# Two parities of a gated mix of attention and FFN: both projected first, or each followed by its own FFN, with weight parts kept in HBM

## The chip, the cores and the metric

The kernel runs on one core of one Trainium2 chip. That core has a matrix engine (PE, with its weight loads PEld), VectorE (DVE), ScalarE (ACT), GpSimd (POOL) and SyncE (SP), which only issues transfers here. Each engine takes its instructions in order and they meet through semaphores. Transfers run on 16 DMA engines; they are issued by SP, by POOL and, in the changed kernel, by ACT. The metric is the device time of one execution in microseconds (us), and the comparison is by the median of several runs.

## The reference

Input x has 2048 tokens of 512 channels, all float32. The output is `g * a + (1 - g) * b`, with attention a and FFN b both computed from x:

```python
x = A_x
g = _sigmoid((x * gate_w).sum(-1, keepdims=True))
# a: 32 heads of 16 channels; token s looks at s, s-2, s-4 ... s-14 (8 places, masked below 0)
logits = jnp.einsum("bhsd,bhswd->bhsw", q, kg) * scale
a = jnp.einsum("bhsw,bhswd->bhsd", softmax(masked logits), vg)  # back to (S, D), then @ wo
b = (_gelu(x @ w_gate) * (x @ w_up)) @ w_down     # F = 1792
out = g * a + (1 - g) * b
```

Since the places looked at are two apart, even and odd tokens never meet in attention. The kernel calls them parity 0 and 1, with 1024 tokens each.

## The kernel before

*Number form.* A float32 product is made of three matmuls of a reduced format: every operand is held as a high part and a low part (what the high part leaves), and high x high, low x high and high x low are added in PSUM. `split` makes the two parts: an ACT copy for the high one, a subtraction on DVE or POOL for the low one (L77). So each product of tiles is three matmuls, 512 columns wide unless said otherwise.

*Projections.* `project(par, cb)` makes, for the 8 token tiles of a parity, one of three column blocks of wqkv: block 0 and 2 are keys and queries of half the heads, block 1 the values of all heads and the gate's sum. `take` (L229) copies a bank of PSUM to SBUF (tags s and r, 3 and 2 buffers) and issues its stores to HBM on SP. The order is written out by hand at the file's end: (0,0), (1,0), (0,1), (1,1), (0,2), (1,2), then `ffn(0)` and `ffn(1)`. x of parity 1 is split and its sums are made early (`load_x1`); the results are put into HBM by POOL (`keep`, 28 stores) and read back by POOL in the first FFN's last step (`operands_1`, 14 reads of 512 KB).

*Attention* runs on DVE: per parity four units of 8 heads. A unit loads keys and queries, makes scores (L289, L291), masks them (a select on POOL, L294), takes the softmax (L302 to L312), multiplies by the values (L325 to L333), transposes, and stores its result to HBM (L340, tensor os, on SP). A generator `fill` holds all units, parity 0 first. `pull(n)` takes about n us of it in between the other work, at a lower priority (`BEHIND`), so that it fills DVE while PE works. The tile framework's scheduler then fixes the order on every engine.

*FFN.* `ffn(par)` goes over 14 blocks f of 128 hidden channels. A product of x with gate and up weights is arranged so that seven products of half size take the place of eight (`gate_up`): it needs sums of weight quarters and sums of x parts (s1 to s4). For each f:
- `fetch` reads gate and up weights (512 KB, tag raw, two buffers) and `fetch_d` the down weights (256 KB, tag r), both on POOL;
- `combine` (L404) forms the differences of quarters, three DVE instructions;
- `operands` makes the high and low parts of the seven weight operands (tags g0, g1, two buffers each): an ACT copy with sign minus into the low part (L420), an accumulating DMA from POOL that adds the raw weight (L421), and an ACT copy into the high part (L423);
- `down_w` splits the down weights, the subtraction on POOL (tag d);
- `gate_up` does the products (L435), copies and additions (L439, L444, L510), the gelu on ACT (L526, L544), the product of gate and up (L448) and its split (L450, L451; the subtraction on DVE for parity 0 and on POOL for parity 1);
- `down` multiplies by the down weights two f at a time (L474). Four token tiles stay in PSUM (`acc`), four go to SBUF and back (L468, L483).

The weights are read, combined and split for parity 0 and once more for parity 1 (`ahead`, `again` prepare f = 0 and 1 of the second FFN during the finish of the first).

*Finish.* The last `down` steps scale by 1 - g (L478), and `finish` adds attention's output times wo (L651) in the same PSUM banks, then copies to SBUF (L660, L662; tags s and rt) and stores the rows (L663, on POOL for parity 0 and SP for parity 1).

*What sets the order around the change:* one queue per engine, the hand-written calls at the end of the file, the scheduler's order within them, and the number of buffers of each tag (`BUFS`).

Of the kernel before, what the change touches and what calls it, by code (L numbers as in the profile page):

```python
# [15 lines left out]
P = 128  # L16
# [14 lines left out]
BT = 4  # L31
# [9 lines left out]
def tile_gated_mix(ctx: ExitStack, tc: tile.TileContext, xt, wqkv, wff, wo, out):  # L41
# [29 lines left out]

    def split(eng, hi, lo, raw, copy=None):
        if copy:
            copy(hi, raw)
        else:
            nc.scalar.activation(hi, raw, AF.Copy)  # L76
        eng.tensor_tensor(lo, raw, hi.bitcast(F32), op=OP.subtract)  # L77


    KS, VS, QS, OS = {}, {}, {}, {}  # L80
# [12 lines left out]
    X, WC = {}, {}  # L93

    def raws():
        for i in range(3):
            if i == 1:
                yield from (tl("c")[:, :512] for _ in range(4))
            else:
                t = tl("raw")  # L100
                yield from (t[:, n * 512:(n + 1) * 512] for n in range(4))

    early = raws()
    for blk in range(2):
        for kc in range(KC):
            X[0, blk, kc] = (tl("rt", F32R), tl("rt", F32R)) if blk and kc < 2 else pair("A")

    def load_xk(kc, blk, first=False):
        hi, lo = X[0, blk, kc]
        for a, n in ((0, P), (P, 512 - P)) if first else ((0, 512),):  # L110
            raw = next(early) if not a else raw
            c = slice(a, a + n)
            nc.sync.dma_start(raw[:, c], xt[blk, :, kc, c])
            split(nc.vector, hi[:, c], lo[:, c], raw[:, c], nc.vector.tensor_copy if first else None)

    def columns():
# [5 lines left out]
        cb0 = of(("g1", 4), ("g1", 4))  # L122
        cb1 = of(("g0", 3), ("g0", 3), ("hh", 1), ("hl", 1))
        for cols in (cb0, cb1):
            for _ in range(KC):
                yield next(cols), next(cols)
# [3 lines left out]
        yield pair("d")  # L130
        yield tl("c", F32R), tl("c", F32R)

    room = columns()

    def load_cb(cb, kc, eng, raw=None):
        hi, lo = WC[cb, kc] = next(room)
        n = 512
        if raw is None:
            raw = next(early) if not cb else tl("c")
            if cb == 1:  # L140
                n = 2 * WQ
                for hh in range(2):
                    nc.sync.dma_start(raw[:, hh * WQ:(hh + 1) * WQ], wqkv[hh, 2, :, kc * WQ:(kc + 1) * WQ])
            else:
# [603 lines left out]
```

## Time and profile before

| | us |
|---|---|
| median of 3 runs | 689.25 (688.2 to 690.62) |
| the profiled execution, its own time | 688.93 |
| its span | 687.2 |
| mean granted PE clock | 0.973 |
| data moved by DMA | 119.64 MB, mean 174 GB/s |

In the rows of the profile, L12 is line 12 of the file, `out<-in` are the program's tile names, `128x512` is partitions x elements, and `x672` is a count of instructions. A group's row gives busy time and the mean of one instruction in ns, then the engine's idle time just before them and what ended it. The table of stages gives each engine's busy time with its count of instructions. DMA share is the busy share of the 16 DMA engines. A row of DMA issues gives the size of one and the median time from issue to landing. A row of waits gives the sum, the number and the longest. The chain of waits follows the work that ended last: start, length, what.

### The profile page before, as it was taken

Reading aid. Unit: us, or ns where it says so; the run is one execution under the profiler, and the core shown is the slowest. Engines: PE = TensorE matmul, PEld = TensorE weight load, DVE = VectorE, ACT = ScalarE, POOL = GpSimd, SP = SyncE. Lnnn points to the kernel's source line nnn. Section 1 sums busy time; section 2 is a strip of 40 time slices with the busy share of each in tenths; the row PEclk is TensorE's granted clock in tenths of the full one; section 3 lists DMA queues with packets and bytes.
Section 4 is the critical chain, followed back from the end, with each engine's and each line's share of the span. In section 5 each row is a group of like instructions: output and inputs, shape, how many; then the busy total and the mean of one; then the engine's idle time right before and its main releaser. Section 6 shows DMA issues by size and latency. Waiting matters only on the chain.

```text
span 687.2 us, 8278 instructions
## 1 busy us (share of the span) xinstructions
PE 635.1 (92%) x2839; PEld 513.2 (75%) x2839; DVE 546.4 (80%) x572; ACT 370.7 (54%) x623; POOL 275.5 (40%) x294
## 2 busy tenths in 40 slices
PE   8899989997999989889999794899898899899997
PEld 7789988885777768668787483687786787678886
DVE  5925998969979898588999995689989999932141
ACT  5523434234666655756566724456674477465561
POOL 5830433005333242324246428437546385453320
PEclk9999999999999999999999997899999999999999
DMA  8999598397574674537578947556645653554123
GB/s 283 325 323 339 172 294 203 100 272 223 129 191 113 141 175 122 137 86 185 124 211 227 385 172 206 174 145 143 185 103 122 154 126 85 130 123 124 31 62 122
DMA packets 70986, 119.64 MB, mean 174 GB/s; under 512 B 7584, under 2 KB 42016, under 8 KB 70944
## 3 DMA queue, kind: packets, MB, share of 16 engines
q0 software_dynamic: 20768, 66.66, 38.5%
q1 hardware_dynamic: 50176, 52.45, 24.4%
q8 instruction: 22, 0.36, 0.2%
q14 instruction: 20, 0.16, 0.1%
HBM read 65.02 MB, written 28.38 MB: 136 GB/s over the span
## 4 chain that ended last, share of the span: by engine, by line
PE 37%; DVE 21%; DMA 18%; issue 11%; ACT 6%; POOL 4%; SPq 2%; DVEq 0%; POOLq 0%; ACTq 0%
PE p L435 22%; PE acc L474 6%; PE p L474 6%; DMA raw<-wff 5%; DVE prod L325 4%; DVE raw L404 3%; DMA g<-raw 2%; DVE prod L329 2%; DMA raw<-xt 2%; DMA raw<-wqkv 2%; PE acc L651 2%; DMA v<-vs 2%; PE p L651 2%; DVE c L448 1%; DVE prod L331 1%
## 5 line engine op out<-in xcount | busy, mean ns | idle before, releaser
L435 PE MATMUL p<-S,g 128*128 128x512 f32 x672 | 176.3, 406 | 15.0 <-ACT p L510 5.8
L435 PEld LDWEIGHTS p<-S,g 128*128 128x128 f32 x672 | 129.8, 195 | 48.9 <-ACT p L510 7.9
L435 PE MATMUL p<-A,g 128*128 128x512 f32 x504 | 135.9, 409 | 20.8 <-DVE c L444 11.8
L435 PEld LDWEIGHTS p<-A,g 128*128 128x128 f32 x504 | 98.1, 197 | 47.6 <-DVE c L444 15.1
L421 POOL DMA_DIRECT2D g<-raw x56 | 50.3, 898 | 157.4 <-ACT g L420 141.7
L325 DVE TENSOR_TENSOR prod<-v,lg 128x2048 f32<-128x2048 f32 x32 | 74.2, 2318 | 6.1 <-DMA v<-vs 5.6
L404 DVE TENSOR_TENSOR raw<-raw 128x256 f32<-128x256 f32 (+1 forms) x84 | 56.7, 677 | 24.9 <-DMA raw<-wff 24.8
L289 DVE TENSOR_TENSOR prod<-k,q 128x2048 f32<-128x2048 f32 x32 | 74.4, 2324 | 1.2 <-DMA qs<-r 1.0
L291 DVE TENSOR_REDUCE lg<-prod 128x128 f32<-128x2048 f32 x32 | 72.9, 2279 | 0.1
L474 PE MATMUL p<-d,hh 128*128 128x512 f32 x224 | 69.6, 398 | 3.1 <-ACT hh L450 1.9
L77 POOL TENSOR_TENSOR d<-r,d 128x512 fp32r<-128x512 f32 x28 | 51.3, 1838 | 33.3 <-ACT d L76 32.5
L420 ACT ACTIVATE g<-raw 128x1024 fp32r<-128x1024 f32 (+1 forms) x56 | 53.2, 950 | 13.1 <-DVE raw L404 10.5
L451 POOL TENSOR_TENSOR hl<-c,hh 128x512 fp32r<-128x512 f32 x28 | 46.0, 1660 | 35.5 <-ACT hh L450 35.3
L393 POOL DMA_DIRECT2D raw<-wff x28 | 21.2, 757 | 95.5 <-DVE S L77 29.7
L450 ACT ACTIVATE hh<-c 128x512 fp32r<-128x512 f32 x56 | 35.4, 632 | 43.4 <-DVE c L448 43.4
L474 PE MATMUL acc<-d,hh 128*128 128x512 f32 x224 | 58.3, 396 | 0.1
L444 DVE TENSOR_TENSOR c<-p,s 128x512 f32<-128x512 f32 x56 | 37.6, 681 | 25.6 <-PE p L435 25.6
L448 DVE TENSOR_TENSOR c<-c 128x512 f32<-128x512 f32 x56 | 44.8, 800 | 14.2 <-ACT c L544 13.6
L474 PEld LDWEIGHTS p<-d,hh 128*128 128x128 f32 x224 | 42.0, 190 | 14.8 <-ACT p L468 2.9
L423 ACT ACTIVATE g<-raw 128x1024 fp32r<-128x1024 f32 (+1 forms) x56 | 53.0, 946 | 0.0
L474 PEld LDWEIGHTS acc<-d,hh 128*128 128x128 f32 x224 | 41.9, 188 | 10.7 <-ACT hh L450 1.1
L483 ACT ACTIVATE rt<-p 128x512 f32<-128x512 f32 x48 | 27.9, 596 | 28.8 <-PE p L474 28.5
(188 smaller groups left out, 1112.8 us busy)
## 6 DMA issues: line engine op xcount, KB each, us to landing
raw<-wff POOLq DMA_DIRECT2D x56, 256.0 KB, 3.5
g<-raw POOLq DMA_DIRECT2D x28, 512.0 KB, 5.1
g<-raw POOLq DMA_DIRECT2D x28, 384.0 KB, 4.5
r<-wff POOLq DMA_DIRECT2D x28, 256.0 KB, 3.1
raw<-xt SPq DMA_DIRECT2D x8, 512.0 KB, 7.1
xs<-S POOLq DMA_DIRECT2D x16, 256.0 KB, 4.6
k<-ks SPq DMA_DIRECT2D x8, 512.0 KB, 5.2
q<-qs SPq DMA_DIRECT2D x8, 512.0 KB, 6.5
```

The source lines that it names most:

```text
L77: eng.tensor_tensor(lo, raw, hi.bitcast(F32), op=OP.subtract)
L289: nc.vector.tensor_tensor(prod, spans(k, jj), q[:, jj:jj + 2, None, :].to_broadcast([P, 2, W, UC]), op=OP.mult)
L291: nc.vector.tensor_reduce(lg[:, jj:jj + 2].rearrange("p j w h -> p (j w h)"), prod.rearrange("p j w (h d) -> p (j w h) d", d=DH), axis=AX. ...
L325: nc.vector.tensor_tensor(prod.rearrange("p j w (h d) -> p j w h d", d=DH), spans(v, jj).rearrange("p j w (h d) -> p j w h d", d=DH), lg[: ...
L404: sub = lambda o, a, b: nc.vector.tensor_tensor(o, a, b, op=OP.subtract)
L420: nc.scalar.activation(lo, raw, AF.Copy, scale=-1.0)
L421: nc.gpsimd.dma_start(lo.bitcast(F32), raw, accum_op=OP.add)
L423: nc.scalar.activation(hi, raw, AF.Copy)
L435: nc.tensor.matmul(ps, w_, a_, start=(start and kc == 0 and n == 0), stop=(kc == 1 and n == 2), skip_group_check=True)
L448: nc.vector.tensor_tensor(ge, ge, up, op=OP.mult)
L451: eng.tensor_tensor(hl_, ge, hh_.bitcast(F32), op=OP.subtract)
L474: nc.tensor.matmul(pp, a[:, ts], w, start=(i == 0 and n == 0 and gr == 0), stop=(i == 1 and n == 2), skip_group_check=True)
```

## The change

1. The order becomes: projections of parity 0, FFN of parity 0, projections of parity 1, parity 0's attention output, FFN of parity 1.

```diff
+    project(0, 1)
+    ...
+    project(0, 2)
+    fetch_d(0)
+    room = rooms()
+    ffn(0)
+    for kc in range(KC):
+        load_cb(1, kc, "c", room)()
+    project(1, 0, sums_x())
+    fetch_o()
+    for kc in range(KC):
+        load_cb(2, kc, "c", room)()
+    project(1, 1)
+    ...
+    for _ in operands(1, 0):
+        pass
     project(1, 2)
-    fetch_d(0)
-    for par in range(2):
-        ffn(par)
+    finish(0, {}, iter(()))
+    ffn(1)
```

2. The first FFN's result, scaled by 1 - g, is stored to the output by itself. Parity 0's attention output is made later in PSUM banks of its own and added to the rows in HBM by accumulating DMAs from POOL.

```diff
-        if gr == NG - 1:
-            jj = BT * b + t
+        jj = BT * b + t
+        if gr == NG - 1 and par:
             nc.scalar.activation(pp, pp, AF.Copy, scale=gc[:, par, jj:jj + 1])
             ACC[jj] = pp
+        elif gr == NG - 1:
+            st = tl("s")
+            nc.scalar.activation(st, pp, AF.Copy, scale=gc[:, par, jj:jj + 1])
+            nc.gpsimd.dma_start(out_v[2 * jj], st)
...
-                    (nc.sync if par else nc.gpsimd).dma_start(out_v[2 * jj + par, :, c], r[:, c])
+                    if par:
+                        nc.sync.dma_start(out_v[2 * jj + par, :, c], r[:, c])
+                    else:
+                        nc.gpsimd.dma_start(out_v[2 * jj, :, c], r[:, c], accum_op=OP.add)
```

3. In the first FFN the finished operands of each f (g0, g1 and d: 0.79, 1.05 and 0.52 MB) are stored to HBM by SP. The second FFN reads them with SP instead of fetching, combining and splitting. In the first FFN the low part of the down weights is made as in `operands`, with an accumulating DMA.

```diff
+            if par:
+                nc.sync.dma_start(w[:, :2 * n].bitcast(F32), WS[f, i])
+                yield
+                continue
             raw = RAW[f][:, (0, 4)[i] * QW:][:, :n]
             nc.scalar.activation(lo, raw, AF.Copy, scale=-1.0)
             nc.gpsimd.dma_start(lo.bitcast(F32), raw, accum_op=OP.add)
             yield
             nc.scalar.activation(hi, raw, AF.Copy)
+            KEEP[f, i] = w[:, :2 * n]
             yield
...
+    def keep(f):
+
+        for i in range(2):
+            w = KEEP.pop((f, i))
+            WS[f, i] = dram.tile(list(w.shape), F32, name=f"ws{f}{i}")
+            nc.sync.dma_start(WS[f, i], w.bitcast(F32))
+        DS[f] = dram.tile([P, 1024], F32, name=f"ds{f}")
+        nc.sync.dma_start(DS[f], WD[f].bitcast(F32))
...
-        split(nc.gpsimd, d[:, :512], d[:, 512:], RD.pop(f))
+        if par:
+            nc.sync.dma_start(d.bitcast(F32), DS[f])
+            return
+        rd = RD.pop(f)
+        nc.scalar.activation(d[:, 512:], rd, AF.Copy, scale=-1.0)
+        nc.gpsimd.dma_start(d[:, 512:].bitcast(F32), rd, accum_op=OP.add)
+        nc.scalar.activation(d[:, :512], rd, AF.Copy)
```

4. x of parity 1 is fetched, split and summed between the FFNs (`fetch_x`, `split_x`, `sums_x`) instead of being saved and reloaded. The blocks of wqkv are read and split for each parity (`load_cb`, `rooms`), 12 more splits. All splits of weights and of wo are on DVE, none on POOL.

5. The stores of `take` are issued by ACT instead of SP:

```diff
-        nc.sync.dma_start(rows(dst[:, W:], jj), two[:, 0])
+        nc.scalar.dma_start(rows(dst[:, W:], jj), two[:, 0])
         if not vals:
-            nc.sync.dma_start(rows(QS[par, hh], jj), two[:, 1])
+            nc.scalar.dma_start(rows(QS[par, hh], jj), two[:, 1])
```

6. The mask is a small constant tile, applied to the one partition that has masked places by a minimum on DVE:

```diff
-        nc.gpsimd.affine_select(out=lg, in_=lg, pattern=[[1, NP], [1, W], [0, UH]],
-                                compare_op=OP.is_ge, fill=MASKED, base=1 - W, channel_multiplier=100)
+        nc.vector.tensor_tensor(lg[:1], lg[:1], mask[:1, :, :, None].to_broadcast([1, NP, W, UH]), op=OP.min)
```

In the new file the operations have these lines: products L411, the low part's copy L380, additions L420, the split's subtraction L427, down products L450, attention times wo L638, the output copy L650, stores of operands L392 and L394, their reads L376 and L399.

297 lines of the change are left out of this document (137 added, 160 removed).

## The prediction

> **What bounds the kernel now.** I read the busy shares first, then the stages, then the chain of waits inside the dearest one, then the DMA queues. The page's first line:
>
> ```profile
> PE 635.1 (92%) x2839; PEld 513.2 (75%) x2839; DVE 546.4 (80%) x572; ACT 370.7 (54%) x623; POOL 275.5 (40%) x294
> ```
>
> The matrix engine PE is never far from busy, so the question is where it loses time. Stages (busy time of each engine with its instructions, granted clock, DMA share, GB/s): both parities' projections; first FFN; its finish; the change of parity; second FFN; finish.
>
> ```profile
> core 0: us, PE busy (x) PEld busy (x) DVE busy (x) ACT busy (x) POOL busy (x), PEclk, DMA share, GB/s
> 0.00:150.50 150.50, 143.00 (x801) 123.79 (x802) 114.92 (x125) 60.42 (x131) 48.28 (x68) 0.99 0.84 259
> 150.50:393.00 242.50, 224.15 (x930) 176.15 (x929) 218.81 (x233) 149.07 (x237) 89.06 (x102) 0.98 0.66 174
> 393.00:415.50 22.50, 21.26 (x91) 16.64 (x89) 22.40 (x21) 7.41 (x12) 9.96 (x8) 1.00 0.50 161
> 415.50:437.00 21.50, 9.36 (x32) 7.16 (x31) 13.22 (x14) 11.54 (x17) 15.71 (x22) 0.74 0.91 270
> 437.00:661.00 224.00, 215.01 (x895) 171.59 (x896) 170.99 (x173) 134.94 (x217) 112.51 (x97) 0.97 0.49 119
> 661.00:687.20 26.20, 22.37 (x97) 17.84 (x95) 6.04 (x10) 7.34 (x13) 0.00 (x0) 1.00 0.25 91
> ```
>
> What PE would need without a wait comes from an undisturbed stretch of the chain:
>
> ```profile
> 675.06 5.55 PE p L651 x24
> ```
>
> That is 0.231 us per matmul of 512 columns. By counts, 930 x 0.231 = 214.8, so the first FFN loses 27.7 of 242.5; the change of parity needs 32 x 0.231 = 7.4 and loses 14.1 of 21.5; the second FFN needs 206.7 and loses 17.3. The finishes lose 1.5 and 3.8 (91 and 97 matmuls). The order of parities can only work on these losses: both kernels issue the same matmuls.
>
> Who PE waits for, and the chain in the change of parity:
>
> ```profile
> PE p L435 <- DVE c L444: 17.0, 9, 3.2
> PE p L435 <- ACT s L662: 9.0, 1, 9.0
> ```
>
> ```profile
> 410.48 5.49 POOL d L77
> ...
> 416.26 5.11 DMA r<-wff
> ...
> 424.51 7.91 PE p L435 x24
> ```
>
> In the FFNs PE waits for VectorE's additions at L444, which stand in line behind attention. At 415.5 it waits 9 us for one ACT copy: ACT has the copy of a down-projection weight ahead of it, and that waits for a fetch which GpSimd could issue only after a 5.49 us subtraction. The granted clock of 0.74 in that stage adds to it.
>
> **The change, part by part.**
>
> *Change of parity.* That chain's three links (fetch, GpSimd subtraction, ACT conversion of a second FFN weight) no longer exist: ready weights come by SP before the second FFN. What can still block ACT is its fourth output copy, L650 in the new file, since tag s has three buffers and each is freed when its output DMA has landed:
>
> ```profile
> out<-s POOLq DMA_DIRECT2D x4, 256.0 KB, 4.6
> ```
>
> From one buffer's copy to the fourth copy PE does six tiles of three matmuls, 18 x 0.231 = 4.2 us, so a plain landing is almost covered. An accumulating one has no row into HBM; into SBUF 512 KB took 5.1 (below), and 13.4 in a crowded stretch. Bounds: a loss of 1 to 10; I take 5, nearer the uncrowded row, half clock included. **Minus 9.**
>
> *Second FFN.* Combinations, conversions, accumulations and weight subtractions go. Per f VectorE is spared one L404 of 0.882 and two of 0.575, 2.0 us, and attention moves in instead: three of parity 1's four units remain after the middle, against about two and a half now. Counting the instructions between the stage's first and last L444 in the built order, at these rows' mean durations, VectorE keeps 173 us against 171. What improves is evenness and two waits:
>
> ```profile
> L404 DVE TENSOR_TENSOR raw<-raw 128x256 f32<-128x256 f32 x56 | 32.1, 575 | 0.1
> ...
> L404 DVE TENSOR_TENSOR raw<-raw 128x512 f32<-128x512 f32 x28 | 24.7, 882 | 24.8 <-DMA raw<-wff 24.8
> ```
>
> VectorE's 24.8 us of waiting for raw weights falls away for parity 1. GpSimd has only the 28 subtractions at L427 left. But SP is in order: a weight read waits for PE to leave its buffer, and attention's loads and stores wait behind it; or it stands itself behind an output store os that waits for VectorE. PE's loss of 17.3 stays whole if the L444 waits stay, and 12 of it goes if only a third do. I take **minus 7**.
>
> *First FFN.* VectorE gets ten splits more (10 x 0.69) and is hindered less:
>
> ```profile
> L77 DVE TENSOR_TENSOR S<-raw,S 128x512 fp32r<-128x512 f32 x16 | 10.6, 687 | 0.0
> ```
>
> ```profile
> L77 POOL TENSOR_TENSOR d<-r,d 128x512 fp32r<-128x512 f32 x28 | 51.3, 1838 | 33.3 <-ACT d L76 32.5 <-PE p L474 0.7
> ```
>
> ```profile
> L448 DVE TENSOR_TENSOR c<-c x56: 676/686/1773, 170.4 to 654.9; 128x512 f32<-128x512 f32 x56
> ```
>
> L448's median is 0.69 and its longest 1.77. The Trainium skill, SBUF — State Buffer, section Who interferes with whom, has an exclusive lock on a port pair when a two-input vector instruction meets a GpSimd instruction that reads SBUF; the spread agrees. With no GpSimd arithmetic left in this stage that speaks for a gain larger than mine; the sum does not use it, and its result is the fast rival.
>
> Against it stands the DMA. Each f now stores 0.79 + 1.05 + 0.52 = 2.36 MB of operands, 33 MB in all, from SP; accumulation for down weights adds 14 x 0.26 = 3.7 MB; x1 and its first weights 3 MB. Gone is the reload of x1's operands, 14 x 0.52 = 7.3 MB.
>
> ```profile
> q0 software_dynamic: 20768, 66.66, 38.5%
> q1 hardware_dynamic: 50176, 52.45, 24.4%
> ...
> raw<-wff POOLq DMA_DIRECT2D x56, 256.0 KB, 3.5
> g<-raw POOLq DMA_DIRECT2D x28, 512.0 KB, 5.1
> ...
> S<-xs POOLq DMA_DIRECT2D x8, 512.0 KB, 10.0
> ...
> A<-xa POOLq DMA_DIRECT2D x6, 512.0 KB, 10.2
> ```
>
> ```profile
> 375.00:400.00 25.00, 19.33 (x78) 1.00 1.05 370
> 380.00:390.00 10.00, 7.65 (x30) 1.00 1.04 410
> ```
>
> A megabyte costs all 16 engines 1.04 / 0.410 = 2.54 us at best, 24.4% x 687.2 / 52.45 = 3.20 on the hardware queue's mean (many rows of 512 bytes), 3.97 on the software queue. Stage now: 0.66 x 242.5 = 160 us. New: 160 + 33 x 2.54 + 3.7 x 3.97 - 7.3 x 2.54 + 3 x 2.54 = 247; at 3.20 the same sum is 267. Over the highest share in a 25 us stretch, 1.05, the DMA alone needs 235 to 254 us, where the stage takes 242.5. Large rows put it near the cheap end. In that crowded stretch landings were:
>
> ```profile
> raw<-wff POOLq DMA_DIRECT2D x4, 256.0 KB, 5.9
> ...
> g<-raw POOLq DMA_DIRECT2D x1, 512.0 KB, 13.4
> ```
>
> So 3.5 becomes 5.9, and 5.1 becomes 13.4. Weights are made a full f ahead (17 us), which covers 13.4; the store of an f has to land within about half an f, or ACT, in order, stops at the next L380 with PE's evacuations behind it. Bounds: 230 (PE with 15 lost) to 270. I take 249, **plus 6.5**: the DMA at its cheap price plus some burstiness.
>
> The Trainium skill, DMA: Bandwidth & Descriptors, section Issuing engines are not separate DMA queues, says that DMAs from all issuing engines run on the same 16 engines and interleave, so giving stores to SP saves only issue time. That speaks against the change, and the crowded landings agree; by it the first FFN is the slow rival's.
>
> *Projections.* Parity 1's follow the first FFN, with eleven or so microseconds of down-projection between. Their twelve weight blocks are split once more on VectorE (12 x 0.69), partly in a middle where by the same count its 95 us of work stand against PE's 101, and parity 0's attention must be done for the first finish. Saving x1 (28 stores) disappears. Issues of stores move from SP to ACT, in front of its copies. No ACT issue is in the trace; SP's took
>
> ```profile
> 40.35 0.44 SPq L238 DMA_DIRECT2D ks<-s  x1
> ```
>
> ```profile
> 48.64 1.30 SPq L240 DMA_DIRECT2D qs<-s  x1
> ```
>
> At 0.44 a copy and two issues need 0.6 + 0.9 = 1.5 us per tile of 12 x 0.231 = 2.8: hidden. At 1.30 it is 3.2, 0.4 too long, and what is late is the freeing of PE's bank. I take 0.44, since x1 stores no longer crowd this part, and for the hand-over **plus 2.5**; bounds minus 3 (less crowding, share 0.84 now) and plus 13 (32 key tiles x 0.4).
>
> *Masking.* A GpSimd select becomes a VectorE minimum on one partition, eight times; at most L448's 0.69 us each, in place of the wait for GpSimd: nothing.
>
> *Sum.* 687.2 - 9 - 7 + 6.5 + 2.5 = 680.2. The profiled execution took 688.93, 1.7 above its span; its median's neighbour is 689.25. So **682**.
>
> **The rivals.**
>
> 1. *The DMA sets the first FFN (slower).* Place: the first FFN. Price: the upper 267 us of DMA work at a sustained share of 0.98, 272, so 23 more than I take: 705. It decides from the point where stores land later than half an f, near a share of 1.0. For it: 13.4 us landings. Against: cheap large rows, and PE kept fed at shares of 0.84 in the projections.
> 2. *VectorE freed, DMA in time (faster).* The first FFN loses 15 instead of 27.7, 230, 19 less than I take: 663. For it: L448's spread. Against: a DMA share near 1.
> 3. *Nothing gained.* The wait for ACT at the change of parity comes back as the wait for a landed accumulation, 14 lost again, the second FFN keeps 5 of the 7, and the first lasts as now: 682 + 9 + 5 - 6.5 = 689.5. For it: three buffers as now. Against: the chain's links are gone.
> 4. *ACT sets the projections (slower)* at 1.30 per issue: 682 + 13 = 695. For it: crowded issues did take that. Against: the 0.44 eight microseconds earlier.
>
> **How the numbers follow.** Forecast 0.42, DMA-set 0.29, fast 0.14, nothing gained 0.09, ACT-set 0.06. This kernel's measurement can tell 0.3%, 2 us, from no change. The forecast's own range, 670 to 692, holds its faster part with 0.34, same 0.04, slower 0.04. Case 3 gives 0.07 to same and 0.02 to slower. So faster 0.48, same 0.11, slower 0.41. The range of 660 to 712 leaves out the ends of cases 1 and 2.
>
> **What would show it.** Right: no gap of 9 us before the second FFN's first products and no ACT wait over 5 us there; DMA share above 0.9 in the first FFN and below 0.6 in the second, the first FFN lasting 244 to 255; no raw-weight wait of VectorE in the second. Wrong: ACT waiting at L380 for stores in the first FFN, or SP's weight reads arriving late behind os stores in the second, or ACT issues over 1 us in the projections.

## The result, and the profile after

The changed kernel takes **663.25 us** (median of four runs, 661.65 to 665.45), against 688.73 for the kernel before beside it: ratio 0.9636, 95% interval 0.9589 to 0.9683. The forecast was 682. The time lies in the range, but the gain is 25 us where 7 were forecast.

Stages of the profile after, columns as in the prediction: parity 0's projections; the hand-over to the first FFN; the first FFN; parity 1's projections; parity 0's finish; the change of parity; the second FFN; the last finish.

```profile
0.00:73.40 73.40, 71.20 (x416) 62.58 (x417) 49.29 (x66) 33.78 (x68) 17.58 (x33) 1.00 0.81 234
73.40:88.00 14.60, 2.57 (x10) 1.80 (x9) 1.56 (x3) 1.89 (x4) 0.00 (x0) 0.72 0.93 351
88.00:334.50 246.50, 230.09 (x962) 180.78 (x961) 217.37 (x258) 163.30 (x263) 63.04 (x87) 0.99 0.91 276
334.50:391.40 56.90, 56.90 (x342) 50.66 (x341) 40.36 (x42) 25.15 (x59) 3.13 (x6) 1.00 0.91 290
391.40:413.70 22.30, 22.30 (x98) 18.09 (x97) 19.54 (x21) 4.67 (x8) 1.77 (x2) 1.00 0.82 264
413.70:438.00 24.30, 19.95 (x74) 15.39 (x73) 21.39 (x19) 7.56 (x12) 8.06 (x7) 0.86 0.86 205
438.00:637.00 199.00, 197.76 (x853) 159.83 (x852) 163.51 (x155) 95.06 (x157) 42.55 (x27) 1.00 0.48 170
637.00:663.60 26.60, 22.53 (x97) 17.90 (x96) 5.51 (x9) 7.40 (x13) 0.00 (x0) 1.00 0.25 89
```

With the prediction's pitch of 0.231 us (0.12 for the projections' 256-column products) each stage's loss follows as before, length minus count times pitch. It holds time in which PE stands idle and time by which matmuls took longer than the pitch:

| PE's loss, us | before | after | difference | forecast |
|---|---|---|---|---|
| projections of both parities | 15.2 | 6.0 - 0.8 = 5.2 | -10.0 | +2.5 |
| hand-over and first FFN | 27.7 | 12.3 + 24.3 = 36.6 | +8.9 | +6.5 |
| change of parity | 14.1 | 7.2 | -6.9 | -9 |
| second FFN | 17.3 | 2.0 | -15.3 | -7 |
| both finishes | 5.3 | 3.9 | -1.4 | 0 |

The differences add to -24.7; the spans differ by 687.2 - 663.6 = 23.6. Two of the four forecast terms are near; the other two are 8 and 12 us off, to the same side.

What PE waits for after, and in the stage with the change of parity what ACT waits for:

```profile
PE p L411 <- ACT r L191: 12.0, 1, 12.0
PE p L411 <- DMA g<-raw: 6.2, 6, 1.7
...
PE p L411 <- DVE c L420: 3.9, 3, 1.6
```

```profile
ACT s L415 <- DMA out<-s: 6.8, 1, 6.8
```

The largest loss is a single one of 12 us, new, at the hand-over. The chain of waits there, and DMA landings of the whole run:

```profile
62.40 7.73 DMA ws<-g
70.15 15.16 DMA qs<-s
85.33 0.37 ACTq L196
```

```profile
ws<-g SPq DMA_DIRECT2D x14, 1024.0 KB, 7.8
...
raw<-wff POOLq DMA_DIRECT2D x28, 256.0 KB, 8.1
g<-raw POOLq DMA_DIRECT2D x14, 512.0 KB, 10.8
```

A row of q, 128 KB in pieces of 512 bytes, lands after 15 us: it has been issued by ACT while SP's first operand stores and GpSimd's fetches fill the DMA engines. ACT, in order, stands for such rows one after the other (10.2 us for the buffer of its copy at 81.4, then until 85.3), and PE needs the bank that a later copy empties. The ACT issue shown took 0.37 us; it is the landing that is dear.

### The profile page after: what moved, and what is told of

Read it like the earlier page. It is cut to its first block, busy times and chain, and to the rows that moved or that the text cites. A ratio compares the mean times of both kernels' runs of the same rounds, so it can differ in the third digit from the quotient of the medians.

```text
span 663.6 us, 8115 instructions
## 1 busy us (share of the span) xinstructions
PE 623.3 (94%) x2839; PEld 507.0 (76%) x2839; DVE 518.5 (78%) x567; ACT 338.8 (51%) x581; POOL 136.1 (21%) x161
## 4 chain that ended last, share of the span: by engine, by line
PE 49%; DMA 26%; DVE 9%; issue 8%; ACT 5%; POOL 2%; ACTq 1%; SPq 0%; POOLq 0%; DVEq 0%
PE p L411 18%; DMA g<-raw 10%; PE p L179 7%; PE acc L179 7%; PE p L450 6%; PE acc L450 5%; PE p L638 3%; PE acc L638 3%; DMA raw<-wff 2%; DMA vs<-s 2%; DMA qs<-s 2%; DMA q<-qs 2%; DMA raw<-xt 2%; DVE prod L281 2%; DMA ws<-g 1%
## 5 line engine op out<-in xcount | busy, mean ns | idle before, releaser
L411 PE MATMUL p<-S,g 128*128 128x512 f32 x672 | 174.1, 400 | 18.9 <-ACT r L191 12.0
L411 PEld LDWEIGHTS p<-S,g 128*128 128x128 f32 x672 | 127.6, 191 | 51.6 <-ACT r L191 12.5
L411 PE MATMUL p<-A,g 128*128 128x512 f32 x504 | 133.4, 399 | 10.2 <-DMA g<-raw 6.2
L411 PEld LDWEIGHTS p<-A,g 128*128 128x128 f32 x504 | 95.0, 190 | 36.4 <-DMA g<-raw 9.4
L427 POOL TENSOR_TENSOR hl<-c,hh 128x512 fp32r<-128x512 f32 x28 | 45.4, 1622 | 160.4 <-ACT hh L426 117.1
L450 PE MATMUL p<-d,hh 128*128 128x512 f32 x224 | 70.0, 401 | 4.9 <-ACT p L444 4.9
L248 DVE TENSOR_REDUCE lg<-prod 128x128 f32<-128x2048 f32 x32 | 73.0, 2281 | 0.3
L450 PE MATMUL acc<-d,hh 128*128 128x512 f32 x224 | 59.1, 395 | 0.0
L450 PEld LDWEIGHTS p<-d,hh 128*128 128x128 f32 x224 | 42.5, 191 | 16.3 <-ACT p L444 6.7
L424 DVE TENSOR_TENSOR c<-c 128x512 f32<-128x512 f32 x56 | 38.4, 685 | 14.7 <-ACT c L523 14.1
L450 PEld LDWEIGHTS acc<-d,hh 128*128 128x128 f32 x224 | 42.0, 188 | 9.9 <-ACT hh L426 0.3
L420 DVE TENSOR_TENSOR c<-p,s 128x512 f32<-128x512 f32 x56 | 38.1, 682 | 13.5 <-PE p L411 13.1
L415 ACT ACTIVATE s<-p 128x512 f32<-128x512 f32 x56 | 32.8, 592 | 26.2 <-PE p L411 19.1
L450 PE MATMUL p<-d,hl 128*128 128x512 f32 x112 | 43.3, 401 | 0.0
L285 DVE TENSOR_TENSOR prod<-prod 128x1024 f32<-128x1024 f32 x32 | 39.5, 1235 | 0.3
L381 POOL DMA_DIRECT2D g<-raw x28 | 26.9, 1009 | 37.4 <-ACT g L380 32.3
L360 DVE TENSOR_TENSOR raw<-raw 128x256 f32<-128x256 f32 (+1 forms) x42 | 21.2, 507 | 16.9 <-DMA raw<-wff 11.6
L380 ACT ACTIVATE g<-raw 128x1024 fp32r<-128x1024 f32 (+1 forms) x28 | 26.6, 950 | 15.3 <-DVE raw L360 12.7
## 6 DMA issues: line engine op xcount, KB each, us to landing
g<-raw POOLq DMA_DIRECT2D x14, 512.0 KB, 10.8
```

The source lines that it names most:

```text
L248: nc.vector.tensor_reduce(lg[:, jj:jj + 2].rearrange("p j w h -> p (j w h)"), prod.rearrange("p j w (h d) -> p (j w h) d", d=DH), axis=AX. ...
L285: nc.vector.tensor_tensor(prod[:, :, :4], prod[:, :, :4], prod[:, :, 4:], op=OP.add)
L411: nc.tensor.matmul(ps, w_, a_, start=(start and kc == 0 and n == 0), stop=(kc == 1 and n == 2), skip_group_check=True)
L420: nc.vector.tensor_tensor(c, ps, s, op=OP.add)
L424: nc.vector.tensor_tensor(ge, ge, up, op=OP.mult)
L427: eng.tensor_tensor(hl_, ge, hh_.bitcast(F32), op=OP.subtract)
```

## The experiments

Times are medians. Each ratio is to the kernel before, run on the same chip beside it.

### The stall at the hand-over

**a_take_sp**: rows of k, q and v issued by SP again.

```diff
-        nc.scalar.dma_start(rows(dst[:, W:], jj), two[:, 0])
+        nc.sync.dma_start(rows(dst[:, W:], jj), two[:, 0])
-            nc.scalar.dma_start(rows(QS[par, hh], jj), two[:, 1])
+            nc.sync.dma_start(rows(QS[par, hh], jj), two[:, 1])
```

> The changed kernel with the stores of k, q and v rows issued by SP again instead of ACT, nothing else. Theory A (the projections lost 10 us less because ACT, no longer waiting in tag s for rows that stand in SP's line behind loads, frees PE's banks in time): the first 73 us lose 10 or more instead of 6, the total is 8 to 12 us longer, about 673. Theory B (they gained because saving x1 and GpSimd's splits are gone): the first 73 us lose 6 as now and the total stays within 2 us of the changed kernel's 663. In the stretch at 73 to 88, where ACT stood 12 us for rows of 512 bytes, theory A expects the stall as long or longer, since the same rows would also stand behind 2.9 MB of operand stores in SP's line; a shorter stall would say that ACT's queue itself was what was slow.

Measured: 656.47, ratio 0.9529 (0.9473 to 0.9586). Neither theory: the change's own part 5 costs 7 us. Windows of the changed kernel and then of this one, 73 to 93 us:

```profile
73.00:93.00 20.00, 7.72 (x27) 5.66 (x26) 6.52 (x9) 4.00 (x7) 0.54 (x1) 0.74 0.88 312
```

```profile
0.00:73.00 73.00, 70.65 (x414) 62.14 (x415) 51.46 (x70) 36.26 (x73) 17.54 (x33) 1.00 0.88 270
73.00:93.00 20.00, 15.54 (x64) 11.49 (x63) 15.94 (x15) 8.72 (x15) 3.69 (x5) 1.00 0.90 267
```

PE does 64 matmuls in place of 27, 37 x 0.231 = 8.5 us. In SP's line the operand stores are issued behind the rows; with two issuers they go out beside them. Between 60 and 100 us the slowest row lands after 8.7 us here, and after 18.3 in the changed kernel. The first 73 us are as good as with ACT (414 matmuls in both), so the issuer is not what the projections gained by.

**a_late_store**: rows by ACT, but the operand stores of f = 0 and 1 wait for that f's first gelu.

```diff
...
+        if not par and f < 2:
+            MARK[f] = pool.tile([1, 2], F32, name="mark", bufs=2)
+            nc.scalar.activation(MARK[f], W_[:1, :2], AF.Copy)
...
+            if f in MARK:
+                nc.sync.dma_start(WS[f, i][:1, :2], MARK[f])
```

> The changed kernel with the operand stores of f = 0 and 1 held back until the first gelu of that f (a mark of two numbers is written ahead of each store into the same place), so that they no longer run beside the last rows of k, q and v. Theory A (the 12.2 us stall of PE at 74.5 comes from those 2.9 MB on the DMA engines): the stall shrinks to 3 us or less, the stretch from 73 to 88 loses 3 instead of 12, total 654 to 657. Theory B (the stall comes from ACT's queue and the fetches of GpSimd and would come anyhow, or the held stores crowd the first f's as much): total within 2 us of 663.

Measured: 654.41, 0.9505 (0.9445 to 0.9565). Theory A: PE's wait of 12.0 us for ACT falls to 1.2, so those stores make that stall. The stretch from 73 to 88 us still loses 15 - 36 x 0.231 = 6.7 us, not 3, and a row of q still takes up to 12.5 us there, so the stores are not the only thing that makes rows late.

**c_both**: both edits together.

> The changed kernel with rows of k, q and v issued by SP and, besides, the operand stores of f = 0 and 1 held back until that f's first gelu. Each alone took 7 to 9 us off (656.5 and 654.4 against 663.3). Theory A (both remove one and the same stall, the operand stores overtaking the last rows: in SP's order they can't, and held back they can't): no further gain, 653 to 658. Theory B (they cure different losses: ACT's queue in the one, the crowd in the other): gains add, 645 to 650.

Measured: 652.04, 0.9467 (0.9413 to 0.9521). A little below theory A's range and above theory B's: mostly one stall. It is 11 us faster than the changed kernel, and the intervals don't meet.

**b_take_act**: the kernel before with rows by ACT.

> The kernel before with the stores of k, q and v rows issued by ACT instead of SP, nothing else. Theory A (my fourth rival's: ACT pays for issues, or stands for its own rows, 8 us in the changed kernel): 691 to 697. Theory B (with no operand stores on the DMA engines the rows land in time whoever issues them; what hurt in the changed kernel was the meeting of the two): within 2 us of 689.

Measured: 686.88, 0.9988 (0.9943 to 1.0034). Theory B: without operand stores beside them, rows by ACT cost nothing that these runs can tell.

### What the stores cost

**a_no_stores**: 13 of the 14 sets of operand stores left out, so that its output is another.

```diff
+            if f:
+                WS[f, i] = WS[0, i]
+                continue
...
+        if f:
+            DS[f] = DS[0]
+            return
```

> The changed kernel, but operands are stored for f = 0 only, and the second FFN reads these copies for every f; 13 of 14 stores, 30.6 MB, are left out, and the output is another. All reads stay. Theory A (the stores crowd the DMA engines and cost the first FFN the 9 us by which it lost more than before, and part of the 12 us stall before it): DMA share of the first FFN from 0.91 to about 0.6, 30.6 x 2.54 = 78 us of DMA work less, the first FFN and the projections together 9 to 15 us shorter, total 648 to 654. Theory B (the stores hide, the first FFN is bound by VectorE, 218 us busy in 246): the share falls as much and the total stays within 3 us of 663. The second FFN should stay at about 2 us lost in both.

Measured: 649.85, 0.9432 (0.9385 to 0.9480). Theory A. Hand-over and first FFN here, then the changed kernel's first FFN cut alike:

```profile
73.00:93.00 20.00, 13.21 (x48) 9.19 (x47) 15.87 (x16) 9.40 (x15) 3.41 (x5) 0.91 0.86 262
93.00:320.20 227.20, 218.49 (x933) 173.83 (x933) 206.26 (x247) 155.22 (x253) 60.09 (x83) 1.00 0.69 168
```

```profile
93.00:334.50 241.50, 225.34 (x947) 177.24 (x946) 212.41 (x251) 161.19 (x259) 62.50 (x86) 0.99 0.92 278
```

The loss falls from 13.8 + 22.7 to 8.9 + 11.7, by 15.9 us (the medians differ by 13.4), and DMA share from 0.92 to 0.69. A store also keeps its weight tile until it has landed; that is in the 15.9.

### Ready weights, or the order?

**a_made_twice**: nothing stored, weights fetched, combined and split again for the second FFN, in the changed order.

```diff
-            if par:
-                nc.sync.dma_start(w[:, :2 * n].bitcast(F32), WS[f, i])
...
-                        if i == 1 and not par and f + 2 < FC:
+                        if i == 1 and f + 2 < FC:
```

> The changed kernel's order of work and side edits, but nothing is stored: the second FFN fetches, combines and splits its weights again, as the kernel before did, with the subtraction of down weights by accumulating DMA. Theory A (the second FFN's loss fell from 17 to 2 us because VectorE no longer makes weights there nor waits for raw ones): the second FFN loses 12 to 17 again, plus 10 to 15, the first FFN gains what the stores cost, 9 to 15, total 655 to 669. Theory B (its loss fell because attention is spread more evenly and GpSimd no longer shares VectorE's port): it loses 2 to 6, and without stores the total is 645 to 655.

Measured: 669.89, 0.9712 (0.9656 to 0.9767), just beyond theory A's range. Its second FFN:

```profile
422.00:642.00 220.00, 208.13 (x873) 164.52 (x872) 188.87 (x187) 145.54 (x236) 98.88 (x99) 0.98 0.62 149
```

It loses 220 - 873 x 0.231 = 18.3, where the changed kernel loses 2.0 and the kernel before 17.3: in this order ready weights save 16 us there, and the order by itself saves nothing. VectorE is busy 188.9 us against 163.5, ACT 145.5 against 95.1.

**c_twice_sp**: the same with rows by SP.

> The changed order with rows issued by SP and nothing stored: the second FFN fetches, combines and splits its weights again. With rows by ACT this was 669.9, against 663.3 with stored operands. Theory A (ready weights give the second FFN its small loss): 662 to 668, that is 6 to 11 more than 656.5 with stored operands, and no better than 660.3 of the kernel before without GpSimd's arithmetic. Theory B (the order by itself is worth the difference between 660.3 and 656.5): 652 to 658.

Measured: 667.5, 0.9639 (0.9487 to 0.9792). The four runs lie between 657.85 and 669.58, so it doesn't decide between the theories.

### GpSimd's arithmetic

The kernel before made masks, splits of projection and finish weights, and the low part of the down weights on GpSimd. These were taken away there, all together (**b_pool_free**) and one by one, order and all else as before.

```diff
b_mask
...
-        nc.gpsimd.affine_select(out=lg, in_=lg, pattern=[[1, NP], [1, W], [0, UH]],
+        nc.vector.tensor_tensor(lg[:1], lg[:1], mask[:1, :, :, None].to_broadcast([1, NP, W, UH]), op=OP.min)
b_d_accum
-        split(nc.gpsimd, d[:, :512], d[:, 512:], RD.pop(f))
+        rd = RD.pop(f)
+        nc.scalar.activation(d[:, 512:], rd, AF.Copy, scale=-1.0)
+        nc.gpsimd.dma_start(d[:, 512:].bitcast(F32), rd, accum_op=OP.add)
+        nc.scalar.activation(d[:, :512], rd, AF.Copy)
b_splits
-            split(nc.gpsimd, hi, lo, raw)
+            split(nc.vector, hi, lo, raw)
...
```

> The kernel before, same order of parities and weights made twice, with GpSimd's arithmetic taken away as in the change: masks as a VectorE minimum, low parts of down weights by accumulating DMA, splits of all projection weights on VectorE. Theory A (what the change gained beside the order comes from GpSimd's arithmetic, which slows VectorE's): projections lose 8 to 10 instead of 15, the second FFN 8 to 12 instead of 17, the change of parity 3 to 5 fewer without the 5.5 us subtraction in its chain; total 668 to 676. Theory B (the gain comes from the order and from reading ready weights): the change of parity gives 3 to 5, the rest nothing or is lost to more VectorE work in the projections; total 683 to 692.

> The kernel before with masks as a VectorE minimum instead of a GpSimd select, nothing else. GpSimd's arithmetic as a whole was worth 28 us (660.3 against 688); which of its three parts carries it is open. Theory A (the select's 8 x 1.56 us and VectorE's wait of 9.1 us for it at L302 count only where PE waits for attention): 0 to 4 us off, 684 to 689. Theory B (attention is the queue that binds, so each microsecond of its waits counts): 8 to 12 off, 677 to 681.

> The kernel before with the low part of the down weights made by ACT and an accumulating DMA instead of GpSimd's subtraction, nothing else: 28 of the 62 GpSimd subtractions outside the masks go, 51 of 120 us. Theory A (shared port, and the 5.5 us subtraction in the chain at the change of parity): VectorE's additions of raw weights fall from a mean of 677 to below 600, the change of parity loses 4 to 8 instead of 14, the total is 12 to 20 shorter, 668 to 676. Theory B (what counts is the splits in the projections): at most 5 off, 683 or more.

> The kernel before with the splits of projection weights that GpSimd made moved to VectorE, nothing else: 11 GpSimd subtractions of 1.6 to 1.8 us less, and so many of 0.69 more for VectorE. Theory A (the projections' loss of 15 is these splits: late on GpSimd, or slowing VectorE): 4 to 8 off, 680 to 684. Theory B (the loss there comes from ACT waiting for its rows and from saved x1, which stay): within 3 us of 688.

| kernel | us | ratio (95%) |
|---|---|---|
| b_pool_free | 660.29 | 0.9580 (0.9518 to 0.9642) |
| b_mask | 682.15 | 0.9899 (0.9827 to 0.9970) |
| b_d_accum | 681.11 | 0.9876 (0.9802 to 0.9950) |
| b_splits | 670.60 | 0.9719 (0.9656 to 0.9781) |

All together they give 28 us, more than theory A expected: **the old order, with nothing stored, is as fast as the changed kernel**, the intervals overlap. The largest part, 11.3 us, is at the change of parity, which loses 22 - 83 x 0.231 = 2.8; the first FFN loses 242.5 - 956 x 0.231 = 21.7, 6 less than before:

```profile
150.50:393.00 242.50, 230.16 (x956) 183.79 (x955) 208.37 (x240) 158.58 (x255) 69.73 (x98) 0.96 0.75 195
...
405.40:427.40 22.00, 19.64 (x83) 15.07 (x82) 18.18 (x14) 12.52 (x22) 14.37 (x19) 1.00 0.98 270
```

One by one, the masks lie between their two theories; the down weights give 8, less than theory A's 12 to 20 and more than theory B's 5; the splits give 18, far over theory A's. (The splits are 16: VectorE's instructions go from 572 to 588; the expectation counted eleven.) Singly they add to 33. Much of each single gain is the same loss, at the change of parity. GpSimd's timeline ahead of it, in the kernel before and in b_splits (start, length, idle before and what ended it):

```profile
391.09 3.18 POOL L77 TENSOR_TENSOR c<-raw,c 128x512 fp32r<-128x512 f32 x1 [4.34 <-DVE hl L451]
...
406.70 0.54 POOL L398 DMA_DIRECT2D r<-wff  x1 [7.32 <-DVE hl L77]
...
410.48 5.48 POOL L77 TENSOR_TENSOR d<-r,d 128x512 fp32r<-128x512 f32 x1 [1.44 <-ACT d L76]
```

```profile
397.46 0.54 POOL L398 DMA_DIRECT2D r<-wff  x1 [3.01 <-DVE hl L77]
401.87 1.29 POOL L77 TENSOR_TENSOR d<-r,d 128x512 fp32r<-128x512 f32 x1 [3.87 <-ACT d L76]
```

```profile
412.80:434.80 22.00, 21.24 (x92) 16.93 (x91) 18.45 (x18) 12.37 (x19) 12.11 (x17) 1.00 0.88 275
434.80:642.40 207.60, 197.72 (x836) 156.98 (x835) 172.68 (x174) 131.04 (x209) 96.84 (x90) 0.99 0.50 123
```

The fetch for the second FFN goes out 9 us earlier (in both it is released by a split of VectorE's; why that came earlier was not followed), the subtraction behind it takes 1.29 us in place of 5.48, and the 22 us after the finish lose 0.7. The second FFN still loses 14.5, with its weights still made there. In b_pool_free it loses 206.8 - 846 x 0.231 = 11.4, 6 less than before:

```profile
427.40:634.20 206.80, 198.80 (x846) 159.03 (x845) 174.34 (x183) 137.05 (x221) 87.50 (x89) 0.99 0.60 143
```

**c_pool_tt** and **c_tt_late** add GpSimd work to the changed kernel with rows by SP.

```diff
c_pool_tt
+        if eng is nc.gpsimd:
+            for _ in range(2):
+                eng.tensor_tensor(junk, junk, junk, op=OP.subtract)
...
c_tt_late
+        if eng is nc.gpsimd:
+            for _ in range(2):
+                eng.tensor_tensor(junk, ge, hh_.bitcast(F32), op=OP.subtract)
...
```

> The changed kernel with rows issued by SP (656.5 us), and in the second FFN two subtractions of 128x512 more on GpSimd behind each one that it makes there, 56 in all, on a tile that nobody else uses; the result is the same. It measures the shared port by itself: no queue waits for these. Theory A (two-input work of GpSimd slows VectorE's): additions at the line of the hidden product rise from 685 ns to a mean of 800 to 950 in that stage, VectorE's 163 us busy there to 180 to 200, PE loses 6 to 17 where it lost 2, total 661 to 672. Theory B (slowed additions are absorbed, since VectorE is idle 36 of the 199 us): total within 2 us of 656.5.

> The changed kernel with rows issued by SP (656.5 us), and in the second FFN each subtraction that GpSimd makes there is made two times more into a tile that nobody reads: 56 of them, some 90 us of GpSimd, where it fetches nothing. In c_pool_tt the same work, free of inputs, had been put at 13 to 169 us; here it reads the hidden product and stays in its place. Theory A (shared port alone): VectorE's additions of the hidden product there rise from 686 to 800 or more, VectorE's 159 us busy in that stage to 175 to 190, PE loses 8 to 20 there instead of 1, total 663 to 676. Theory B (GpSimd costs time only by its queue, where fetches stand behind its arithmetic): VectorE slows but PE loses at most 2 more, total within 3 us of 656.5.

c_pool_tt measured 669.04, 0.9701 (0.9623 to 0.9778), but the work, which waits for nothing, had been put at 13 to 169 us, into the projections and the first FFN, where GpSimd also fetches: 12.6 us, with two possible reasons. c_tt_late keeps it in the second FFN, where GpSimd fetches nothing: 682.06, 0.9936 (0.9897 to 0.9975), 25.6 us more than 656.47, beyond theory A's range. Windows of the second FFN, first without and then with it, and VectorE's groups in the same order:

```profile
435.00:628.00 193.00, 191.84 (x827) 154.65 (x826) 157.35 (x150) 93.49 (x154) 39.35 (x26) 1.00 0.49 170
```

```profile
435.00:655.00 220.00, 201.57 (x829) 158.83 (x828) 188.29 (x150) 94.11 (x158) 129.68 (x78) 0.96 0.42 150
```

```profile
L248 DVE TENSOR_REDUCE lg<-prod 128x128 f32<-128x2048 f32 x9 | 20.5, 2281 | 0.1
L246 DVE TENSOR_TENSOR prod<-k,q 128x2048 f32<-128x2048 f32 x9 | 20.5, 2277 | 0.1
L424 DVE TENSOR_TENSOR c<-c 128x512 f32<-128x512 f32 x25 | 17.2, 686 | 10.9 <-ACT c L523 10.5
L420 DVE TENSOR_TENSOR c<-p,s 128x512 f32<-128x512 f32 x24 | 16.2, 679 | 12.1 <-PE p L411 12.0
```

```profile
L246 DVE TENSOR_TENSOR prod<-k,q 128x2048 f32<-128x2048 f32 x9 | 24.4, 2710 | 0.1
L424 DVE TENSOR_TENSOR c<-c 128x512 f32<-128x512 f32 x25 | 21.5, 861 | 10.1 <-ACT c L528 9.8
L248 DVE TENSOR_REDUCE lg<-prod 128x128 f32<-128x2048 f32 x9 | 20.5, 2279 | 0.1
L420 DVE TENSOR_TENSOR c<-p,s 128x512 f32<-128x512 f32 x25 | 16.9, 678 | 12.1 <-PE p L411 12.0
```

The same 150 VectorE instructions take 31 us longer, and the stage's loss rises by 26.5 (28.5 in place of 2.0): 25.6 / 56 = 0.46 us of kernel time per subtraction. Of the 26.5, 17.3 are time in which PE is idle (18.4 in place of 1.2); the other 9 are matmuls that took longer, at a granted clock of 0.96. VectorE's 36 us of idle time absorbed next to nothing, because 22 of them lie in the last 33 us, when attention is done; before that VectorE is busy 146.3 of 160 us:

```profile
595.00:628.00 33.00, 33.00 (x144) 26.72 (x143) 11.05 (x16) 19.93 (x36) 5.74 (x5) 1.00 0.17 56
```

Operations that read two tiles slow down. In the whole run of c_tt_late, the 47 products at L424 that met no subtraction on GpSimd took 0.68 us on average, the 8 that overlapped one by 0.3 us or more took 1.46. The reduction (2281 and 2279 ns), which reads one tile, and L420, which reads one of its two inputs from p, PE's bank, don't slow down. The Trainium skill, SBUF — State Buffer, section Who interferes with whom, says just this: a vector instruction with two SBUF inputs contends with a GpSimd instruction that reads SBUF, one with at most one does not, outside the vector engine's 2-port modes. The trace agrees line by line. The added work also holds its inputs some 3 us longer; in this stage PE waits 0.8 us for a result of GpSimd, and ACT and VectorE for none, so that can only be a small part.

**a_d_pool**: in the changed kernel, the down weights' low part on GpSimd again, in the first FFN. **c_both_d_pool**: the same on top of c_both. The edit is that of b_d_accum, backwards.

> The changed kernel with the low part of the down weights subtracted on GpSimd again (14 subtractions of 128x512, 1.84 us each by the profile of before), instead of by an accumulating DMA. Theory A (GpSimd's two-input arithmetic slows VectorE: before, additions of 685 ns took up to 1.77 us): the additions of the first FFN, mean 685 ns now, rise to 750 to 800, VectorE's 217 us busy in the first FFN rise by 5 to 15, total 667 to 675. Theory B (the slowed additions don't bind, and 3.7 MB of accumulation fewer help the DMA): total within 3 us of 663.

> The changed kernel with rows by SP, operand stores of f = 0 and 1 held back (652.0 us together), and the low part of the down weights subtracted on GpSimd in the first FFN. Theory A (the accumulating DMA of the down weights crowds the DMA engines in the first FFN, and GpSimd's subtraction costs less): another 3 to 6 off, 646 to 649. Theory B (its 6 us came only from the stall at 74 us and the change of parity, which the two other cures shorten too; the port costs as before): 652 to 658.

Measured: 656.89, 0.9543 (0.9482 to 0.9604), and 651.21, 0.9489 (0.9415 to 0.9563). Neither falls into either of its theories: a_d_pool's median is 6 us below the changed kernel's, and the intervals just touch. The products of gate and up (L421 there) do slow down, from 685 to 765 ns, as theory A had it, but with the accumulation's writes gone the DMA share is 0.87 in place of 0.92 and 93 to 327.6 us lose 17.7 in place of 22.7:

```profile
93.00:327.60 234.60, 222.24 (x939) 176.18 (x940) 213.64 (x246) 152.43 (x245) 73.97 (x83) 0.99 0.87 269
```

So there the price of GpSimd's arithmetic is smaller than the accumulation's. On top of c_both, 651.21 against 652.04, the two come out even, although the DMA share of its first FFN is 0.96; what decides between the two cases was not tried.

**c_o_pool**: the finish's weights split on GpSimd in the changed kernel with rows by SP (in `load_o`, `nc.vector` becomes `nc.gpsimd`; four splits for each of the two finishes).

> The changed kernel with rows issued by SP (656.5 us), and the four splits of the finish's weights back on GpSimd. In the kernel before, eleven splits of this kind and of projection weights moved to VectorE took 18 us off, 16 of them at the change of parity. Theory A (in the old order they delayed GpSimd's fetches for the second FFN; in the new order GpSimd has none to make there): within 3 us of 656.5. Theory B (the splits themselves are late, or slow VectorE's output splits and copies): 5 or more longer, lost at the change of parity.

Measured: 654.83, 0.9526 (0.9439 to 0.9612), theory A: in the new order, where GpSimd has no fetch for the second FFN to make, the splits on GpSimd cost nothing that these runs can tell.

### The projections

**b_no_x1**: the kernel before with one pair of saves of x1 in place of 14, so that its output is another.

```diff
+        if XS:
+            XS[n, kc] = next(iter(XS.values()))
+            return
         x = XS[n, kc] = dram.tile([P, 1024], F32, name=f"x{n}{kc}")
```

> The kernel before, but of the 28 saves of parity 1's operands (14 of them pairs, 7.3 MB) only the first pair is made, and the second FFN reads this pair in place of the others; 13 pairs are left out and the output is another. Theory A (the saves crowd the DMA engines and GpSimd's queue while rows of k, q and v have to land, and ACT waits for these): the projections, where PE lost 10.5 us in gaps, lose 5 or less, total 681 to 684. Theory B (what costs there is the preparation of both parities' operands on VectorE and ACT beside parity 0's projections, which stays): they lose 8 or more, total 685 to 690.

Measured: 669.78, 0.9745 (0.9692 to 0.9797). Theory A for the projections, and more in total. The first 73 us before and here, and the first and last start of the FFNs' products:

```profile
0.00:73.00 73.00, 68.33 (x377) 58.07 (x378) 45.55 (x61) 33.09 (x65) 29.17 (x52) 1.00 0.95 310
```

```profile
0.00:73.00 73.00, 70.72 (x400) 60.97 (x401) 57.68 (x73) 38.72 (x78) 27.42 (x35) 1.00 0.80 248
```

```profile
L435 PE MATMUL p<-A,g x504: 387/394/794, 150.2 to 653.8; 128*128 128x512 f32 x168
```

```profile
L438 PE MATMUL p<-A,g x504: 387/393/632, 142.6 to 636.9; 128*128 128x512 f32 x168
```

What ACT waits for most among its rows of k, q and v in the first 150 us, before and here:

```profile
ACT r L235 <- DMA qs<-r: 11.2, 3, 7.7
```

```profile
ACT s L238 <- DMA vs<-s: 8.4, 4, 3.2
```

The first FFN begins 7.6 us earlier, and DMA share falls from 0.95 to 0.80. All waits of ACT for its rows to land fall from 30.0 to 14.6 us. The rest of the 17 us is again at the change of parity, where 85 matmuls fall in the 22 us after the finish. In b_mask these are 71, in b_d_accum 83, in b_splits 92, of 95 that PE could do. That loss was thus a meeting of late events, which four different edits take away for more than half; so the single gains can't be added.

## Why the prediction was wrong, point by point

**Second FFN, -7 forecast, -15.3 measured: a failed step.** What failed is the pricing of the loss: all 17.3 us were put on PE's waits for VectorE's additions at L444, of which more than a third were to stay. But 17.0 us is the sum of these waits over the whole run; in this stage they were 5.7. What PE waits for there, before and after:

```profile
PE p L435 <- DVE c L444: 5.7, 3, 2.1
PE p L435 <- ACT p L510: 3.0, 2, 2.7
PE acc L474 <- POOL hl L451: 0.3, 1, 0.3
```

```profile
PE p L411 <- DVE c L420: 1.2, 1, 1.2
```

So of the 17.3 only 224 - 215.01 = 9.0 is time in which PE stands; the other 8.3 are matmuls that took longer than the pitch, at a granted clock of 0.97, a term put at nothing. In the first 38 us of the stage, for one, PE stands 0.3 us and loses 38 - 151 x 0.231 = 3.1, at a clock of 0.92, right behind the long wait at the change of parity; that the clock falls because PE stood was not tested. After, the clock is 1.00, the waits for ACT are gone (it was busy 134.9 us with weights to convert, and is 95.1 without), and one wait for an addition is left. The 24.8 us for which VectorE waited for raw weights were a figure of the whole run too; 9.3 of them were in this stage.

The forecast that VectorE's work stays the same did hold. From the first addition of the second FFN to the last, before and after:

```profile
439.98:650.89 210.91, 201.92 (x845) 160.98 (x845) 166.28 (x168) 126.06 (x200) 107.04 (x93) 0.98 0.49 118
```

```profile
426.88:626.92 200.04, 198.80 (x849) 160.52 (x848) 167.61 (x155) 90.93 (x149) 43.67 (x27) 0.99 0.51 177
```

VectorE is busy 167.6 us against 166.3. (The 163.5 and 171.0 of the tables of stages can't be compared: the window after holds 26 of the 28 additions, the one before all.) So it was not the rows' mean durations that misled, although they contain what GpSimd's arithmetic added: L448 took 842 ns on average in this stage, its counterpart L424 686.

That ready weights do it is shown by a_made_twice: in the same order, with weights made in the stage, 18.3 us are lost again, with waits of 6.5 for additions and 5.0 for ACT. Which part counts, VectorE's combinations, ACT's conversions or the fetches, was not separated. In the old order GpSimd's arithmetic has a price there too. At c_tt_late's 0.46 us per subtraction, the 14 for the down weights are worth 14 x 0.46 = 6.4 us, an estimate; b_pool_free, where they are gone together with masks and splits, lost 17.3 - 11.4 = 5.9 less. The two gains don't add: a_made_twice has none of these subtractions either.

**Projections, +2.5 forecast, -10 measured: a failed step.** It was named ("saving x1 disappears") and bounded at minus 3. b_no_x1 shows 7.6 for the saves alone: with them, ACT stood 30.0 us for its rows to land, without them 14.6, and PE's waits for ACT's copies fell from 5.6 to 0.2. What the other 2.4 are was not separated. The second half of the term, rows issued by ACT, was sized by issue time (0.44 or 1.30). The 96 issues took 0.45 at the median, as forecast, and five of them over 1 us; the cost was a landing of 15 us. It appeared at the hand-over, in the next line of the table, and is worth 7 (a_take_sp).

**Hand-over and first FFN, +6.5 forecast, +8.9 measured.** The DMA share is above 0.9, and GpSimd's landings went from 3.5 and 5.1 to 8.1 and 10.8, as forecast. That the size came out near is luck in part, since two misses offset each other. a_no_stores prices the stores at 15.9 us, more than twice the term. And 7.1 came back for which the sum had nothing: without stores 20.6 would be lost, 27.7 were lost before. That is the second rival's mechanism, a less hindered VectorE, and b_pool_free shows 6.0 of it in the old order. The form was not foreseen: a third of the loss is one stall. By the Trainium skill, DMA: Bandwidth & Descriptors, section Issuing engines are not separate DMA queues, all issuers' transfers interleave on the same engines; the 15 us landing agrees, and a_take_sp adds what one queue still gives, an order.

**Change of parity, -9 forecast, -6.9 measured.** Right within its bounds. ACT waits 6.8 us for an accumulating landing, the third rival's mechanism; that is inside the 1 to 10 given, but over the 5 us that were to show the prediction right. And ready weights were not needed for the gain: b_splits loses 0.7 there.

**The rivals.** The second had the time (663) with another account, so its hit is luck: the first FFN did not shrink. The DMA-bound first FFN, with 0.29 the strongest rival, was half true: the DMA did bind at times, but at the cheap price per megabyte. Its busy time from 73 us to the end of the first FFN differs between the changed kernel and a_no_stores by 0.88 x 20 + 0.92 x 241.5 - 0.86 x 20 - 0.69 x 227.2 = 66 us for 30.6 MB, 2.15 each. The fourth's place lost nothing: PE is busy all of the 56.9 us of parity 1's projections.

**What the change is worth by its parts.** GpSimd's arithmetic alone gives the old order 28 us. In the changed order ready weights win 16 in the second FFN and pay up to 16 in stores; as a whole the changed kernel is 6.6 us faster than a_made_twice. Against b_pool_free the order with stores comes out ahead when the stall is cured: 656.5 with rows by SP, where the intervals still overlap, and 652.0 with late stores as well, where they just touch. Whether the order without stores is worth anything stays open (c_twice_sp).

## What to carry to other kernels

The loss of a stage belongs to the waits of that stage. A sum over the whole run that happens to match it (17.0 and 17.3) proves nothing: ask for the waits window by window, and set idle time apart from work that took longer. A mean duration, too, contains what its neighbours added. And when an edit bundles a large plan with small side edits, run the side edits alone on the old kernel first: they gave as much as the whole change, and the plan came out ahead of them once one of the side edits had been taken back.

## What the runs showed of the hardware that was not expected

GpSimd slows down as well: one subtraction of 128x512 took from 1.29 to 5.48 us. In the kernel before, the 18 of its subtractions that overlapped two-input work of VectorE by less than 0.1 us took 1.33 us on average, the 45 that overlapped it by 0.6 us or more took 1.96. And small rows on one queue can land after 18 us while megabyte stores go out on another, though the median is 2.7 (q) and 3.8 us (k and v); issued on the same queue as those stores, ahead of them, they took 5.5 us at the median and at most 8.7 (changed kernel and a_take_sp, 60 to 100 us).
